# Fewer dummy matmuls, an earlier first weight magnitude, half of the first state sums moved behind two units, and eight matmuls split, in a scan that feeds a gated MLP

## The chip, the cores and the metric

The kernel runs on one core of a Trainium2 chip. The metric is the device time of one execution in microseconds (us); lower is better. The engines are PE (TensorE, with PEld for its weight loads), DVE (VectorE), ACT (ScalarE), POOL (GpSimd) and SP (SyncE, which here issues most of the DMAs).

## The reference

A scan over 768 tokens in chunks (4 batches, 8 heads, state 16, head width 32) gives an output that is laid out as 3072 rows of 256 values, and a gated MLP works on these rows. Cut to what matters:

```
log_a = log(clip(a, 1e-6, 1))                       # a: (4, 8, 768)
for each chunk of 32 tokens:
    cum = cumsum(log_a[chunk])
    L = exp(cum_i - cum_j) * (i >= j)
    M = (C @ B^T) * L
    y[chunk] = M @ x + (C @ state) * exp(cum)
    state = exp(sum(log_a)) * state + sum_j B_j x_j * exp(cum_end - cum_j)
x = y as (3072, 256)
out = (silu(x @ w_gate) * (x @ w_val)) @ w_out      # 256 -> 1536 -> 256
```

## The kernel before

**Tiling.** The tokens are taken in 6 blocks (`NB`) of 128 tokens, each of all four batches, so that a block has T = 512 columns. A block k goes through the scan first: the decays L (`scan_spread`, `scan_j`), the scores S (`scores`), the mix of the two (`mix`), the values, the carried states and the sums for new states on PE; the result is x of the block. Then it goes through 12 units f of the MLP. A unit computes gate and value (`gate_val`, m = 0 and 1, the tiles gv), silu on ACT, the product on DVE, and a high and a low half of that product (`hid_high`, `hid_low`) for the output sums (`project`, the tiles po).

**State sums.** The chunk of the scan is 64 tokens wide here, two pieces q of a block. Each piece has its own sum over B and x (`sums_of_pieces`, tile st for block 0). `apart` copies a piece's sum, by heads, from PSUM into the tile T, and `step` brings T of the second piece up to date with the first by the decays E. The values and carried matmuls of the first block stand in `values_first` and `carried_first`, and read T of the first piece alone; block 1 carries on from the second.

**Weights.** `w_gate` and `w_val` arrive as twelve pieces wg0 to wg11, one for each unit, `w_out` as wo0 to wo5. A piece of raw data (wg0r) is prepared in steps: its magnitude (ACT), range (POOL for the pieces in `FAR`, wg0 among them, else DVE), shift, sign and round (DVE), and a rest (ACT). The first nine units of block 0 (`WHOLE`) use the whole piece (wg0w) with the whole x (xf): two fp32 matmuls for each half unit m, which PE does as four passes. All others are three products of a high and a low half, six matmuls for each half unit (lines 652 to 654). Of the first piece, the gate half is rounded first, then the value half, in two operations each.

**Order.** A planner (`Plan`) takes all operations with an engine, a cost, a rank, needs and buffers, and puts them into an order by ranks, costs and due times (`due`). `plan.follow(...)` and the table `ORDER` fix chains of operations on an engine by hand. What comes out is one instruction stream for each engine, which that engine keeps to. All instructions are recorded by one helper, so every row says L191.

**Dummies.** `idle` issues matmuls whose result nobody reads: nine groups of four, 64 columns wide, at the start, and one 512 columns wide behind `e` (`IDLE`, lines 967 and 968). In the trace they write the tile rest.

**DMA.** SP loads B and C (bc), x and B by tokens (xb), the decays and the weight pieces wg. The clipped logarithms of all blocks are written to memory by ACT (clipped<-all), and L and E of the later blocks are loaded from there. POOL issues accumulating transfers, which make the low halves wg0l and so on, and xl of block 0.

Names of the tiles in rows: st, y and S are PSUM tiles of the scan; e is the spread decay that E is copied from.

Of the kernel before, what the change touches and what calls it, by code (L numbers as in the profile page):

```python
# [22 lines left out]
Q = 64  # L23
K = P // Q
T = BATCH * P
# [176 lines left out]
def scan_moe_kernel(ctx: ExitStack, tc, aj, an, bc, xb, wgv, wo, cst, own, first_e, out):  # L202
# [35 lines left out]
    def piece(q):  # L238
        return slice(Q * q, Q * q + Q)
# [180 lines left out]
    def sums_of_pieces(k, b):  # L420

        c = bl[k]
        if not b:
            tiles = c["tiles"][::2] if k else banks(k, "st", K)
            half = slice(BATCH * Q, None) if k else slice(0, BATCH * 2 * D)
            c["st"] = [t[:, half].rearrange("p (b c) -> p b c", c=2 * D) for t in tiles]
        for p in range(NP):
            for q in range(K - last(k, K - 1)):
                o = 2 * D * (p ^ b % 2)
                te.matmul(  # L430
                    c["st"][q][pair(p), b], c["Bj"][piece(q), b, pair(p)],
                    c["x"][piece(q), b, o : o + 2 * D], start=not k, stop=True, skip_group_check=k > 0,
                )

    def new_states(k):
        bl[k]["T"] = att.tile([P, K, BATCH, 2 * D], F32, tag="T", name=f"T{k}", bufs=2)
# [208 lines left out]
    def gate_val(k, f, m):  # L645
        t = hid.setdefault((k, f), {})["gv"[m]] = ps_mm.tile([P, T], F32, tag="mm", name=f"gv{k}_{f}_{m}")
        if not k and f < WHOLE:
            w = part[f]["w"].bitcast(F32).rearrange("p (a b c) -> p a b c", b=2, c=P)
            for kc in range(2):
                te.matmul(t, w[:, m, kc], whole[0][:, kc], start=not kc, stop=kc == 1)  # L650
            return
        runs = [(w, x, kc) for w, x in PASSES[not k] for kc in range(2)]
        for i, (w, x, kc) in enumerate(runs):
            te.matmul(t, w[f][:, m, kc], x[k][:, kc], start=i == 0, stop=i == 5)

    def silu(k, f):
        t = hid[k, f]
# [76 lines left out]
    def do(f, *a):  # L734
        return lambda *e: f(*a, *e)
# [78 lines left out]
    for k in range(NB):  # L814
# [44 lines left out]
        for bs in [(b,) for b in range(BATCH)] if not k else [range(BATCH)]:  # L859
            b, more = bs[-1], bs[0]  # L860
            n = len(bs)
            if not k:
                add("PE", 0.2, do(sums, 0, bs), -1.5, [("bt", 0), *([("st", 0, more - 1)] if more else [])], takes=[] if more else [("at", i) for i in st], uses=st, gives=("st", 0, b), kind="f")
            add("PE", 0.43 if n == 1 else 1.8, do(scores, k, bs), z + 3.5 if k else -1.9 + 0.1 * b, [("Cz", k)] + ([("S", k, more - 1)] if more else []), takes=[] if more else [("at" if k else "mm", i) for i in S], uses=[*S, CZ], gives=("S", k, b), kind="f", slack=SLACK)
        done = [("S", k, BATCH - 1)]
        add("-", 0.0, do(new_states, k), z + 2, behind("T"), takes=[("T", TT)], gives=("T", k))
        for q in range(len(st)):
            add([("Act", 0.65), ("DVE", 0.36)] if k else "Act", None if k else 0.65, do(apart, k, q) if k else do(apart, 0, q, "Act"), r + 2 if k and q else z + 4 + 0.5 * q, [("st", k, BATCH - 1), ("T", k)], uses=y if k else [st[q]], gives=("ap", k, q))
# [44 lines left out]
    for k in range(NB):  # L913
# [36 lines left out]
    plan.follow([  # L950
        *(("spread", b, 0) for b in range(BATCH)),
        *(("spread", b, 1) for b in range(BATCH)), *(("S", 0, b) for b in range(BATCH)),
        "e", *(("idle", 1, i) for i in range(len(IDLE[1]))), *(("st", 0, b) for b in range(BATCH)),
        ("vals", 0), ("y", 0, 0), ("vals", 1), ("y", 0, 1),
    ])
    plan.follow([("raw", i) for i in range(NW)])
    for steps in ORDER:
        plan.follow(steps)
    plan.follow([("clip", 0), ("clip", 1), "row"] + [("L", 0, b) if i else ("scan0", b) for b, i in halves] + [("bt", 0), ("M", 0, 0), ("M", 0, 1), ("ce", 0), ("M", 0, 2), ("M", 0, 3), ("shift", 0), ("sign", 0, "gate"), ("round", 0, "gate"), ("sign", 0), ("round", 0), ("step", 0, 1), ("range", 1)])
    plan.STAY = {"Act": 0.0, "PE": 0.3}  # L960
    plan.issue()

# [1 line left out]
CST = 2 + 2 * D  # L964
E_ROWS = slice(64, 64 + BATCH * H)
NA = NB * K * BATCH * H // P
IDLE = [-9.0] * 9, [-4.0]
IDLE_AFTER = [], ["e"]
FIRST_X = 0, 1, 2, 3, 4, 5
FETCH = dict(aj=10.0, an=35.0, bc=12.0, xb=31.0)  # L970
LATER = 3.0
WHOLE = 9
LAST = (5, 6, 9, 10, 11, 12)
MINUS = (3, 3, 4, 5, 5, 5, 10, 10, 10)
FEW = 8
# [2 lines left out]
SLOW = {2: 9.0}  # L978
ORDER = (
    ["few", ("raw", 2)],  # L980
    [("range", 2), "products", ("sign", 2)],
    [("mag", 6), "written e", ("rest", 7)],
    [("raw", 8), ("bc", 1), ("raw", 9), ("aj", 1), ("raw", 10), ("xb", 1), ("raw", 11), ("E", 1)],
    [("E", 0), ("mag", 0), ("ap", 0, 0), ("ap", 0, 1), ("rest", 0), *(("xf", i) for i in FIRST_X)],
    [("xf", 5), ("mag", 1), ("rest", 1), ("mag", 2), ("rest", 2), ("mag", 3)],
    [("round", 1), ("range", 2)],
    [("si", 0, 2), ("Cz", 1)],
# [64 lines left out]
```

## Time and profile before

| | us |
|---|---|
| median of 3 runs | 348.28 (347.66 to 348.31) |
| the profiled execution | 350.54 |
| its span, from the first instruction to the last | 348.5 |
| PE busy in the span | 341.0 |
| DVE busy | 224.4 |
| ACT busy | 124.8 |
| POOL busy | 45.1 |

The span is what the profiler's views count from; every time in a row is counted from its start. The profiled execution is one of its own and is not among the three timed runs. An engine that is busy for nearly the whole span sets the time in most places; the places where it is not busy are found in the timeline and in the chain of waits.

### The profile page before, as it was taken

The page shows a single profiled execution, that of the slowest core. Times are in us where ns is not written, and L with a number is a line of the kernel's source. Part 1 is how long each engine was busy: PE and PEld are TensorE (multiplying, and loading weights), DVE is VectorE, ACT ScalarE, POOL GpSimd, SP SyncE. Part 2 cuts the span into 40 slices and gives each one's busy share as a digit, 9 for nine tenths or more (in the row PEclk, how much of TensorE's full clock was granted, in tenths as well). Part 3 has the DMA queues.
Part 4 walks back from the last instruction along what each step waited for, and adds up shares of the span by engine and source line. Part 5 has one row for each costly group of instructions (what it writes and reads, how often), then busy time and mean ns, then how long its engine had stood idle before and what let it go on. Part 6 is the DMA issues. An engine that isn't in the chain of part 4 may idle for free.

```text
span 348.5 us, 7432 instructions
## 1 busy us (share of the span) xinstructions
PE 341.0 (98%) x3207; PEld 267.1 (77%) x3207; DVE 224.4 (64%) x398; ACT 124.8 (36%) x233; POOL 45.1 (13%) x36
## 2 busy tenths in 40 slices
PE   8979999999999999999999999999999999999996
PEld 7534448888878888888888888888888888888895
DVE  7869999969899882686472677445676430565320
ACT  4659958563355412222322222321212221222221
POOL 2366836410222000000000000000000000000000
PEclk9989999999999999999999999999999999999999
DMA  7799887992000951000471000391000000100001
GB/s 253 255 374 177 252 205 150 267 241 73 1 2 13 206 151 61 0 2 2 141 167 60 0 2 2 98 179 74 20 0 3 2 2 0 60 2 0 0 2 60
DMA packets 9983, 30.98 MB, mean 89 GB/s; under 512 B 1311, under 2 KB 2111, under 8 KB 9311
## 3 DMA queue, kind: packets, MB, share of 16 engines
q1 hardware_dynamic: 7192, 24.23, 24.8%
q0 software_dynamic: 1440, 2.88, 4.7%
q10 hardware_dynamic: 1319, 3.41, 3.3%
q8 instruction: 25, 0.41, 0.5%
q14 instruction: 7, 0.06, 0.1%
HBM read 24.28 MB, written 3.35 MB: 79 GB/s over the span
## 4 chain that ended last, share of the span: by engine, by line
PE 96%; DVE 2%; ACT 1%; DMA 1%; issue 0%; ACTq 0%; DVEq 0%
PE gv L191 59%; PE po L191 28%; PE y L191 4%; PE S L191 2%; PE a L191 1%; DVE wg1w L191 1%; DMA rows<-in_aj 1%; DVE wg0w L191 0%; PE e L191 0%; PE st L191 0%; DVE T L191 0%; DVE wg2w L191 0%; ACT T L191 0%; ACT xf L191 0%; ACT wg0r L191 0%
## 5 line engine op out<-in xcount | busy, mean ns | idle before, releaser
L191 DVE TENSOR_TENSOR sg<-gv,sg 128x512 f32<-128x512 f32 x72 | 49.5, 688 | 78.8 <-PE gv L191 75.7
L191 ACT ACTIVATE sg<-gv 128x512 f32<-128x512 f32 x72 | 42.8, 597 | 105.1 <-PE gv L191 105.1
L191 DVE TENSOR_TENSOR hh<-sg,hh 128x512 fp32r<-128x512 f32 x72 | 49.9, 695 | 13.2 <-ACT hh L191 11.7
L191 ACT CAST hh<-sg 128x512 fp32r<-128x512 f32 x31 | 19.3, 623 | 26.6 <-PE po L191 18.8
L191 DVE TENSOR_TENSOR_SCAN L<-L,dj 128x520 f32<-128x520 f32 x20 | 23.9, 1242 | 3.0 <-DMA L<-clipped 3.0
L191 ACT COPY ob<-po 128x512 f32<-128x512 f32 (+1 forms) x13 | 7.2, 555 | 48.6 <-PE po L191 48.1
L191 DVE CAST hh<-sg 128x512 fp32r<-128x512 f32 x41 | 17.3, 425 | 2.0 <-PE po L191 0.8
L191 PE MATMUL po<-hh,wo4h 128*128 128x512 f32 (+1 forms) x52 | 15.2, 376 | 0.0
L191 PE MATMUL po<-hh,wo2h 128*128 128x512 f32 (+1 forms) x52 | 15.2, 376 | 0.0
L191 PE MATMUL po<-hh,wo0h 128*128 128x512 f32 (+1 forms) x52 | 15.2, 375 | 0.0
L191 DVE TENSOR_TENSOR L<-S,L 128x512 f32<-128x512 f32 x24 | 15.0, 681 | 0.1
L191 PE MATMUL po<-hh,wo5h 128*128 128x512 f32 (+1 forms) x52 | 15.1, 373 | 0.0
L191 PE MATMUL po<-hh,wo1h 128*128 128x512 f32 (+1 forms) x52 | 15.0, 373 | 0.0
L191 PE MATMUL po<-hh,wo3h 128*128 128x512 f32 (+1 forms) x52 | 15.0, 373 | 0.0
L191 PEld LDWEIGHTS po<-hh,wo0h 128*128 128x128 f32 x52 | 9.5, 188 | 1.9 <-issue 0.2
L191 PEld LDWEIGHTS y<-L,xb 64*32 64x32 f32 x768 | 9.0, 109 | 2.6 <-issue 1.8
L191 PE MATMUL y<-L,xb 64*32 64x64 f32 x768 | 10.9, 231 | 0.0
L191 PEld LDWEIGHTS po<-hh,wo5h 128*128 128x128 f32 x52 | 9.5, 188 | 1.7
L191 PEld LDWEIGHTS po<-hh,wo1h 128*128 128x128 f32 x52 | 9.5, 188 | 1.7
L191 PEld LDWEIGHTS po<-hh,wo3h 128*128 128x128 f32 x52 | 9.5, 188 | 1.7
L191 PEld LDWEIGHTS po<-hh,wo4h 128*128 128x128 f32 x52 | 9.4, 188 | 1.8
L191 PEld LDWEIGHTS po<-hh,wo2h 128*128 128x128 f32 x52 | 9.4, 188 | 1.8
(302 smaller groups left out, 750.2 us busy)
## 6 DMA issues: line engine op xcount, KB each, us to landing
L<-clipped SPq DMA_DIRECT2D x10, 520.0 KB
xb<-in_xb SPq DMA_DIRECT2D x6, 768.0 KB, 10.5
bc<-in_bc SPq DMA_DIRECT2D x6, 512.0 KB, 3.3
out<-ob SPq DMA_DIRECT2D x11, 256.0 KB, 6.0
E<-clipped SPq DMA_DIRECT2D x5, 260.0 KB
wg0r<-in_wgv SPq DMA_DIRECT2D x1, 512.0 KB
wg1r<-in_wgv SPq DMA_DIRECT2D x1, 512.0 KB
wg2r<-in_wgv SPq DMA_DIRECT2D x1, 512.0 KB
```

What stands on the lines that cost most here:

```text
L191: ins = getattr(self.engine, name)(*a, **k)
```

## The change

Five things change. The nine groups of dummies at the start become four, 16 matmuls for 36. The state sums of block 0 are split by piece: `first_sums(0)` stays where both were, `first_sums(1)` has a PSUM bank of its own and needs the second half of unit 1, gv(0, 1, 1). The copy of the second piece into T (`apart`) and T's step follow later. ACT's list has the magnitude of wg0 ahead of E's copy. The third chain in `ORDER`, which places the list of products among DVE's steps, has other neighbours. In unit 6 of block 1 (`HALVED`), the middle four of six matmuls of each half unit are done in two halves of 256 columns: eight matmuls become sixteen.

```
-            tiles = c["tiles"][::2] if k else banks(k, "st", K)
-            half = slice(BATCH * Q, None) if k else slice(0, BATCH * 2 * D)
+            half = slice(BATCH * Q, None)
 ...
+    def first_sums(q):
+        t = banks(0, f"st{q}", 1)[0][:, : BATCH * 2 * D]
+        bl[0].setdefault("st", {})[q] = t.rearrange("p (b c) -> p b c", c=2 * D)
+        for b in range(BATCH):
+            for p in range(NP):
+                sum_of(0, b, q, p)
 ...
-            te.matmul(t, w[f][:, m, kc], x[k][:, kc], start=i == 0, stop=i == 5)
+            n = T // 2 if (k, f) == HALVED and 0 < i < 5 else T
+            for o in range(0, T, n):
+                te.matmul(t[:, o : o + n], w[f][:, m, kc], x[k][:, kc, o : o + n], start=i == 0, stop=i == 5)
 ...
+        for q in range(K if not k else 0):
+            add("PE", 0.45, do(first_sums, q), due(0, 1) if q else -1.5, [("bt", 0), *([("gv", 0, 1, 1)] if q else [])], takes=[("at", st[q])], uses=[st[q]], gives=("st", 0, q), kind="f")
 ...
-... r + 2 if k and q else z + 4 + 0.5 * q, [("st", k, BATCH - 1), ("T", k)], ...
+... r + 2 if k and q else due(0, 5) if q else z + 4, [("st", k, BATCH - 1 if k else q), ("T", k)], ...
 ...
-        "e", *(("idle", 1, i) for i in range(len(IDLE[1]))), *(("st", 0, b) for b in range(BATCH)),
+        "e", *(("idle", 1, i) for i in range(len(IDLE[1]))), ("st", 0, 0),
 ...
-    ... ("sign", 0), ("round", 0), ("step", 0, 1), ("range", 1)])
+    ... ("sign", 0), ("round", 0), ("range", 1)])
 ...
-IDLE = [-9.0] * 9, [-4.0]
+IDLE = [-9.0] * 4, [-4.0]
+HALVED = 1, 6
 ...
-    [("range", 2), "products", ("sign", 2)],
+    [("round", 3), "products", ("sign", 4)],
-    [("E", 0), ("mag", 0), ("ap", 0, 0), ("ap", 0, 1), ("rest", 0), *(("xf", i) for i in FIRST_X)],
+    [("mag", 0), ("E", 0), ("ap", 0, 0), ("rest", 0), *(("xf", i) for i in FIRST_X)],
```

On PE, the order around the first units, before (y is the scan's last work on block 0, and gv0_1_0 is the first half of unit 1 of block 0):

```order
L191 MATMUL y10_2_341<-bc0_98,T0_113 64x64 x2
L191 MATMUL gv0_0_0_397<-xf_142,wg0w_248 128x512 x2
L191 MATMUL gv0_0_1_414<-xf_142,wg0w_248 128x512 x2
L191 MATMUL gv0_1_0_426<-xf_142,wg1w_394 128x512 x2
L191 MATMUL gv0_1_1_438<-xf_142,wg1w_394 128x512 x2
L191 MATMUL gv0_2_0_456<-xf_142,wg2w_410 128x512 x2
L191 MATMUL gv0_2_1_472<-xf_142,wg2w_410 128x512 x2
```

And with the change (st10 is the sum of the second piece):

```order
L191 MATMUL y10_2_306<-bc0_98,T0_113 64x64 x2
L191 MATMUL gv0_0_0_357<-xf_140,wg0w_227 128x512 x2
L191 MATMUL gv0_0_1_372<-xf_140,wg0w_227 128x512 x2
L191 MATMUL gv0_1_0_384<-xf_140,wg1w_355 128x512 x2
L191 MATMUL gv0_1_1_395<-xf_140,wg1w_355 128x512 x2
L191 MATMUL st10_0_406<-xb0_100 32x64 x16
L191 MATMUL gv0_2_0_427<-xf_140,wg2w_367 128x512 x2
L191 MATMUL gv0_2_1_449<-xf_140,wg2w_367 128x512 x2
```

The 16 matmuls of the second piece's sums, which stood ahead of the values of block 0, now stand between units 1 and 2.

On DVE, the order behind the rounding of the first piece, before (ISA is the rounding, which the trace calls CUSTOM_DVE_ANT_0; T<-T,E is T's step, sg0_0 the product of unit 0):

```order
L191 ISA wg0w_248<-wg0r_138,wg0w_248 128x512
L191 SCALAR_TENSOR_TENSOR T0_113<-T0_113,E0_97 128x64 x4
L191 TENSOR_SCALAR wg1w_394<-wg1w_394 128x512 x2
L191 SCALAR_TENSOR_TENSOR wg1w_394<-wg1r_151,wg1w_394 128x512
L191 ISA wg1w_394<-wg1r_151,wg1w_394 128x1024
L191 TENSOR_SCALAR wg2w_410<-wg2w_410 128x512
L191 SCALAR_TENSOR_TENSOR all_102<-all_102,dn_82 128x195
L191 TENSOR_SCALAR wg2w_410<-wg2w_410 128x512
L191 TENSOR_TENSOR sg0_0_418<-gv0_0_1_414,sg0_0_418 128x512
```

And with the change, the same place up to the product of unit 1 (without the round of wg0, which is followed by the first of these rows):

```order
L191 TENSOR_SCALAR wg1w_355<-wg1w_355 128x512 x2
L191 SCALAR_TENSOR_TENSOR wg1w_355<-wg1r_143,wg1w_355 128x512
L191 ISA wg1w_355<-wg1r_143,wg1w_355 128x1024
L191 TENSOR_SCALAR wg2w_367<-wg2w_367 128x512 x2
L191 TENSOR_TENSOR sg0_0_375<-gv0_0_1_372,sg0_0_375 128x512
L191 SCALAR_TENSOR_TENSOR wg2w_367<-wg2r_167,wg2w_367 128x512
L191 ISA wg2w_367<-wg2r_167,wg2w_367 128x1024
L191 TENSOR_SCALAR wg3w_378<-wg3w_378 128x512
L191 SCALAR_TENSOR_TENSOR wg3w_378<-wg3r_172,wg3w_378 128x512
L191 ISA wg3w_378<-wg3r_172,wg3w_378 128x1024
L191 SCALAR_TENSOR_TENSOR all_102<-all_102,dn_82 128x195
L191 TENSOR_TENSOR sg0_1_398<-gv0_1_1_395,sg0_1_398 128x512
```

T's four steps are no longer between wg0 and wg1; they are the next row behind the last one here. The scan of all later blocks' logarithms (all<-all,dn) has moved from wg2 to behind wg3.

On POOL, the order of the ranges of wg8 to wg10 and of the accumulating DMAs, before:

```order
L191 TENSOR_SCALAR wg8w_490<-wg8w_490 128x512
L191 TENSOR_SCALAR wg9w_519<-wg9w_519 128x512
L191 DMA wg0l_511<-wg0w_248 128x512
L191 DMA wg1l_530<-wg1w_394 128x512
L191 TENSOR_SCALAR wg10w_555<-wg10w_555 128x512
L191 DMA wg2l_540<-wg2w_410 128x512
L191 DMA xl0_401<-xf_142 128x1024
```

And with the change:

```order
L191 TENSOR_SCALAR wg8w_461<-wg8w_461 128x512
L191 DMA wg0l_493<-wg0w_227 128x512
L191 DMA wg1l_499<-wg1w_355 128x512
L191 TENSOR_SCALAR wg9w_509<-wg9w_509 128x512
L191 DMA wg2l_522<-wg2w_367 128x512
L191 TENSOR_SCALAR wg10w_575<-wg10w_575 128x512
L191 DMA xl0_361<-xf_140 128x1024
```

Two DMAs have come ahead of the range of wg9, and one ahead of that of wg10. In block 1, one of the two copies of sums into T stands on DVE where it stood on ACT. SP's order of DMAs is the same.

## Rows read from the trace of the kernel before

**Rows 1.** The page: engines' busy us (share of the span) xinstructions; queues' packets, MB, share.
```profile
PE 341.0 (98%) x3207; PEld 267.1 (77%) x3207; DVE 224.4 (64%) x398; ACT 124.8 (36%) x233; POOL 45.1 (13%) x36
...
q8 instruction: 25, 0.41, 0.5%
```

**Rows 2.** The chain that ended last: start us, us, what.
```profile
2.83 0.42 DVE rows L191
...
18.40 0.69 DVE wg1w L191
19.10 0.76 DVE wg2w L191
19.97 20.74 PE gv L191 x44
...
225.81 16.32 PE po L191 x72
...
328.42 16.87 PE po L191 x108
```

**Rows 3.** Timeline of PE, 15.2 to 24: start, us, what [idle before <-releaser].
```profile
15.31 1.96 PE L191 MATMUL gv<-xf,wg0w 128*128 128x512 f32 x4 [0.38 <-ACT xf L191]
19.97 3.42 PE L191 MATMUL gv<-xf,wg0w 128*128 128x512 f32 x4 [2.71 <-DVE wg2w L191]
```

**Rows 4.** Timeline of DVE, 11 to 20.
```profile
13.70 0.43 DVE L191 TENSOR_SCALAR wg0w<-wg0w 128x512 int32<-128x512 int32 x1 [0.86 <-POOL wg0w L191]
...
15.88 0.86 DVE L191 SCALAR_TENSOR_TENSOR T<-T,E 128x64 f32<-128x64 f32 x4
```

**Rows 5.** Timeline of all engines and queues, 16 to 46.
```profile
16.68 0.19 PEld L191 LDWEIGHTS gv<-xf,wg0w 128*128 128x128 f32 x1 [0.24 <-issue]
...
25.31 0.35 ACTq L191 DMA_DIRECT2D clipped<-all  x1
...
37.55 1.02 POOL L191 DMA_DIRECT2D wg0l<-wg0w  x1
37.63 0.67 SPq L191 DMA_DIRECT2D E<-clipped  x1
```

**Rows 6.** Windows: busy us (xinstructions) by PE, PEld, DVE, ACT, POOL; clock; DMA; GB/s.
```profile
0.00:19.90 19.90, 15.69 (x347) 11.34 (x348) 16.22 (x36) 12.38 (x30) 6.38 (x12) 1.00 0.78 273
19.97:23.60 3.63, 3.63 (x5) 1.54 (x5) 0.77 (x3) 1.08 (x2) 3.63 (x3) 0.53 1.02 417
19.09:39.83 20.74, 19.86 (x43) 8.71 (x43) 16.89 (x30) 16.09 (x30) 15.78 (x9) 0.92 1.01 264
39.80:63.75 23.95, 23.95 (x382) 14.95 (x381) 23.88 (x43) 17.38 (x36) 13.91 (x11) 1.00 0.84 205
```

**Rows 7.** DMA view, 17.0 to 19.9: queue, packets, MB, share of 16 engines.
```profile
q8 instruction: 1, 0.02, 2.0%
```

**Rows 8.** DMA view, 19.9 to 37.9 (of its three queues, the first and the last).
```profile
q1 hardware_dynamic: 1065, 4.57, 99.8%
...
q14 instruction: 2, 0.02, 0.2%
```

**Rows 9.** Timelines of PE, at other places.
```profile
11.14 1.15 PE L191 MATMUL st<-xb 64*32 64x64 f32 x62
...
26.82 3.60 PE L191 MATMUL gv<-xf,wg2w 128*128 128x512 f32 x8
30.25 3.60 PE L191 MATMUL gv<-xf,wg3w 128*128 128x512 f32 x8
...
64.01 0.63 PE L191 MATMUL gv<-xh,wg0h 128*128 128x512 f32 x2
```

**Rows 10.** Timeline of ACT, 9 to 16.
```profile
10.99 0.69 ACT L191 ACTIVATE wg0w<-wg0r 128x512 f32<-128x512 f32 x1
12.62 0.88 ACT L191 ACTIVATE T<-st,cs 128x128 f32<-128x128 f32 x3
```

**Rows 11.** Timeline of DVE, 38 to 41: the first scans of block 1.
```profile
39.75 2.73 DVE L191 TENSOR_TENSOR_SCAN L<-L,dj 128x520 f32<-128x520 f32 x2
```

More of the change, by code (lines that the diff above doesn't have):

```diff
@@ L423, in sums_of_pieces, with sum_of @@
         if not b:
-            tiles = c["tiles"][::2] if k else banks(k, "st", K)
-            half = slice(BATCH * Q, None) if k else slice(0, BATCH * 2 * D)
-            c["st"] = [t[:, half].rearrange("p (b c) -> p b c", c=2 * D) for t in tiles]
+            half = slice(BATCH * Q, None)
+            c["st"] = [t[:, half].rearrange("p (b c) -> p b c", c=2 * D) for t in c["tiles"][::2]]
         for p in range(NP):
             for q in range(K - last(k, K - 1)):
[L429 to L433, printed above, removed]
+                sum_of(k, b, q, p)
+    def sum_of(k, b, q, p):
+        c = bl[k]
+        o = 2 * D * (p ^ b % 2)
+        te.matmul(
+            c["st"][q][pair(p), b], c["Bj"][piece(q), b, pair(p)],
+            c["x"][piece(q), b, o : o + 2 * D], start=not k, stop=True, skip_group_check=k > 0,
+        )
+    def first_sums(q):
[4 more added lines that the diff above has]
+                sum_of(0, b, q, p)
     def new_states(k):
@@ L861, in scan_moe_kernel @@
             n = len(bs)
-            if not k:
-                add("PE", 0.2, do(sums, 0, bs), -1.5, [("bt", 0), *([("st", 0, more - 1)] if more else [])], takes=[] if more else [("at", i) for i in st], uses=st, gives=("st", 0, b), kind="f")
             add("PE", 0.43 if n == 1 else 1.8, do(scores, k, bs), z + 3.5 if k else -1.9 + 0.1 * b, [("Cz", k)] + ([("S", k, more - 1)] if more else []), takes=[] if more else [("at" if k else "mm", i) for i in S], uses=[*S, CZ], gives=("S", k, b), kind="f", slack=SLACK)
@@ L866, in scan_moe_kernel @@
         add("-", 0.0, do(new_states, k), z + 2, behind("T"), takes=[("T", TT)], gives=("T", k))
+        for q in range(K if not k else 0):
+            add("PE", 0.45, do(first_sums, q), due(0, 1) if q else -1.5, [("bt", 0), *([("gv", 0, 1, 1)] if q else [])], takes=[("at", st[q])], uses=[st[q]], gives=("st", 0, q), kind="f")
         for q in range(len(st)):
-            add([("Act", 0.65), ("DVE", 0.36)] if k else "Act", None if k else 0.65, do(apart, k, q) if k else do(apart, 0, q, "Act"), r + 2 if k and q else z + 4 + 0.5 * q, [("st", k, BATCH - 1), ("T", k)], uses=y if k else [st[q]], gives=("ap", k, q))
+            add([("Act", 0.65), ("DVE", 0.36)] if k else "Act", None if k else 0.65, do(apart, k, q) if k else do(apart, 0, q, "Act"), r + 2 if k and q else due(0, 5) if q else z + 4, [("st", k, BATCH - 1 if k else q), ("T", k)], uses=y if k else [st[q]], gives=("ap", k, q))
         for p in range(NP):
@@ L958, in scan_moe_kernel @@
         plan.follow(steps)
-    plan.follow([("clip", 0), ("clip", 1), "row"] + [("L", 0, b) if i else ("scan0", b) for b, i in halves] + [("bt", 0), ("M", 0, 0), ("M", 0, 1), ("ce", 0), ("M", 0, 2), ("M", 0, 3), ("shift", 0), ("sign", 0, "gate"), ("round", 0, "gate"), ("sign", 0), ("round", 0), ("step", 0, 1), ("range", 1)])
+    plan.follow([("clip", 0), ("clip", 1), "row"] + [("L", 0, b) if i else ("scan0", b) for b, i in halves] + [("bt", 0), ("M", 0, 0), ("M", 0, 1), ("ce", 0), ("M", 0, 2), ("M", 0, 3), ("shift", 0), ("sign", 0, "gate"), ("round", 0, "gate"), ("sign", 0), ("round", 0), ("range", 1)])
     plan.STAY = {"Act": 0.0, "PE": 0.3}
```

## The prediction

> **What bounds the kernel now.** I read the page first: TensorE (PE) is busy 341.0 of 348.5 us, 98% [rows 1]. The chain of waits says where the other two per cent lie: from 19.97 us on it is PE work nearly to the end, and ahead of that it runs through the preparation of the first weight pieces on VectorE, wg1w, then wg2w [rows 2]. So whatever is won must be won before PE runs free, and kept until the next place where PE waits. The timeline of PE shows the one large hole: the first half of unit 0 (four passes) ends at 17.26, the next four start at 19.97, 2.71 us later [rows 3]. The view names wg2w's preparation as the releaser. But the matmul behind the hole reads xf and wg0w; it takes nothing from wg2. VectorE had rounded its weights before T's step, which stands behind that round, began at 15.88 [rows 4], and its weight load had already begun at 16.68 [rows 5]; the engine had its data and stood still. What was missing? The windows count 347 matmuls and 348 weight loads up to 19.90, so the one that stands still is about number 695 of PE's stream [rows 6]. The page has a queue that carries nothing but instructions: 25 packets, 0.41 MB; PE's 6414 instructions over 25 packets are 257 a packet [rows 1]. One such packet moved between 17.0 and 19.9, while the hole lasted [rows 7], and none at all between 19.9 and 37.9, when the data queue held the DMA engines for 99.8% of the time [rows 8]. I take the hole for PE waiting for its own instructions, which came late because the DMA engines were full. What follows it costs too: from 19.97 to 23.60 the granted clock is 0.53, near the lower of TensorE's two levels, after an idle stretch [rows 6]; the four passes took 3.42 us, where eight take 3.43 from one unit's start to the next later on (26.82 to 30.25) [rows 9], so 1.71 for four: 1.7 us more.
>
> [...]
>
> **The change, part by part.** *20 dummies fewer.* They stand ahead of `a`, and the chain comes to `a` through VectorE's work on its rows, to 3.25, and not through them [rows 2]: 0; with that cover gone, fewer dummies could only let it start earlier. What counts is that the stream gets 40 instructions shorter (a load and a matmul each).
>
> *Half of the first sums moved.* 64 passes took 1.15 us at 11.14 [rows 9]; 32 of them, with their 32 loads, go behind two units. ScalarE then has two copies of T instead of four ahead of its work on wg0 and xf: 0.88/3 = 0.3 each [rows 10], some 0.6 us on ScalarE, of which I let 0.4 count since it also waits for y. The hole's instruction, number 695, is now 40 + 64 = 104 further on. Counting eight instructions for each half unit, unit 0's second half, unit 1 and the 64 sums fill 88 of these, unit 2 the 16 left: it is now the first of unit 3.
>
> *Magnitude of wg0 first.* It ran at 10.99, behind E's copy [rows 10]. Its data can't be dated by a row; I take 0.9 us earlier, and from 0 to 1.3 as bounds. GpSimd's range of wg0 goes with it, and VectorE's shift waited 0.86 us for that range, from 12.84 to 13.70 [rows 4]; so 0.86 of the 0.9 count. Round 0 ends at 15.0 instead of 15.9. E's copy comes up to 0.3 later; its readers on VectorE have that slack.
>
> *T's step moved.* Its four pieces, 0.86 us on VectorE [rows 4], stood between round 0 and wg1's preparation. Now they stand behind product 1. Round 1 ended at 19.09 [rows 2]; 0.86 and half of the 0.86 above, less what ScalarE's magnitude of wg1 takes back, make 18.1. The copies' reader, the carried part of block 1, comes over 20 us later: 0 there.
>
> *So the start becomes:* unit 0 at 14.9 (15.31 less 0.4) to 18.3, at 3.43 us for a unit; unit 1 from 18.4 (round 1, 18.1, and a hop) to 21.8; the moved sums between 0 and 0.58, half of 1.15: I take 0.3; unit 2 at 22.1 where it was 26.82 [rows 9]. That is 4.7 us. The hole is gone if the packet lands before unit 3, 25.5. No row shows when it is asked for. If it is asked for one packet earlier in the stream, at number 439, that was within the sums, at about 11.4, before [rows 9], and it came by 19.9, 8.5 us; in the changed kernel that number comes at about 13, so it would land at 21.5, 4 us early. The other bound is in the rivals.
>
> *Two matmuls of four split in unit 6 of block 1.* Eight matmuls become sixteen halves. In the last sums, 36 whole and 72 half ones take 16.87 us, in the ones before 72 whole ones 16.32, 0.2267 each [rows 2]; so a half takes (16.87 - 36 x 0.2267)/72 = 0.121 and a pair 0.015 more than a whole: 8 x 0.015 = 0.12 us. [...]
>
> **What is late next.** The 4.7 us arrive at block 1's decays on VectorE, not at the end. From 19.09 to 39.83 VectorE is busy 16.89 of 20.74 us [rows 6]; from 18.1 on, with the step's 0.86, it could be through at 35.9 instead of 39.75, when the scans of L(1) begin [rows 11]. But L(1) must have landed. It has no landing row; the ends are 35.9 (already there) and 39.75 (it is what the scan waited for). The nearest row is ScalarE's write issued at 25.31, behind L's loads: its landing let SyncE issue E at 37.63 [rows 5]. I take 37.0: 2.75 earlier. From 39.80 to 63.75 VectorE is busy 23.88 of 23.95 us [rows 6], so its work there is the bound and PE's first pass on block 1 at 64.01 [rows 9] hangs on it, moving as it moves. One copy of T in block 1 now falls to VectorE, at most the 0.43 of a shift of 512 columns [rows 4]; I take 0.35: 64.01 - 2.75 + 0.35 = 61.6, a gain of 2.4, not 4.7: the rest goes into PE's wait for block 1. From there PE is the bound. Less 0.12 for the split: 2.3.
>
> **How it stands to the times.** The profiled run took 350.54 us, of it 348.5 in the span; the median of the timed runs is 348.28, 2.26 less. In the profiled run's own terms I forecast 348.2. Whether the timed runs have the low clock after the hole too, nothing shows; without it their scans would begin up to 1.6 us earlier and the gain be 2.3 - 1.6 = 0.7. I take a quarter of that off: 1.9, or **346.4 us**. With L landed early the scans start at 35.9, 3.85 earlier, and the gain is 3.85 - 0.35 - 0.12 = 3.4: 344.9.
>
> **Rivals.** *A: L(1) comes no earlier, or later.* On GpSimd the accumulating transfers of wg0l and wg1l, issued from 37.55 before [rows 5], now stand ahead of wg9's range instead of behind it, and so start earlier, in the stretch in which the DMA engines are full [rows 8]. For it: that share, 99.8%. Against: L's loads are queued well ahead of them, before the write of 25.31. If L lands at 39.75 as before, the gain is 0, and the copy and the split cost 0.35 + 0.12; less 0.1 to 0.2 where they are hidden: 348.6. It decides from a landing at 38.6 on, where under 0.7 is left.
>
> *B: the hole isn't instructions.* If the view is right and the matmul is let go by wg2's range, that ends 0.76 us behind round 1 [rows 2], at 18.9, and the second half starts at 19.0 instead of 19.97: 1.0 earlier, less 0.3 for the sums and 0.12: 347.7. For it: the releaser named, and the times fit (19.86 and 0.11). Against: that matmul reads nothing of wg2, and a hole that ends with an instruction packet needs no second reason. [...]
>
> *C, slower: the packet is late at its new place.* The rows show 18.0 us without a single packet, 19.9 to 37.9 [rows 8], under the same load that the changed kernel has when PE comes to unit 3. If the packet asked for at about 13 isn't through before this stretch, it comes when the data queue falls idle: PE stands from 25.5 to 37.9 and starts unit 3 at 38.0 at the earliest, where it was 30.25 [rows 9]: 7.8 us later, 356.0. It decides from a landing at 30.2 on; with 18 us of delay alone, 31, it would be about 1 us slower. Against: asked for no later than 1 us behind its time before, it should come nearly as then.
>
> [...]
>
> **How the numbers follow.** What this kernel's measurement can tell from no change is about 0.2%, 0.7 us (347.6 to 349.0). The forecast has a chance of 0.66 (faster 0.61, and 0.05 within 0.2%, where the timed runs have no low clock); A 0.12 (0.09 within, 0.03 slower, where the new transfers delay L past 39.75); B 0.10 (0.08 within, 0.02 faster); C 0.12, slower. Together: faster 0.63, same 0.22, slower 0.15. The range runs from 344.9 (L early) to 348.6 (A) and leaves out C and tails, some 0.2.
>
> **What would show it.** The profile after should have no hole in unit 0, a granted clock near 1 from 15 to 25, unit 2 at about 22, an instruction packet well before 25, the scans of L(1) at about 37 and PE on block 1's xh at 61.6. A hole ahead of unit 3 means C; one that has stayed in unit 0 and ends with wg2's range means B; scans that wait for L until 39 mean A. I'd be wrong altogether if PE reached block 1 two us early and lost them again further on, at weights of wg9 to wg11 or at xl, whose loads and accumulating transfers I have only bounded as unchanged.

## The result, and the profile after

The changed kernel takes 350.33 us in the median of 12 runs (348.98 to 351.02); the kernel before takes 348.29 beside it. The ratio is 1.0054, with an interval of 1.0039 to 1.0070: 2.0 us slower. The prediction was 346.4, in a range of 344.9 to 348.6, and faster. The time lies outside the range and on the other side.

The profiled execution after took 349.17 us, 1.4 less than the 350.54 of the profiled one before. Both numbers mislead, in opposite ways. The one after stands at the lower edge of its 12 runs. The one before stands 2.26 above the median of its own: it belongs to a few executions with a mean granted clock of 0.994 or 0.995, 6 of 35 of the kernel before and none of the 12 after. So both kernels were profiled once more. Four profiles, by the starts of PE's pieces, in us:

| | before, as shown | before again | after, as shown | after again |
|---|---|---|---|---|
| time of the execution | 350.54 | 348.33 | 349.17 | 350.39 |
| unit 0 | 15.31 | 15.75 | 15.39 | 15.52 |
| unit 1 | 23.19 | 21.15 | 19.13 | 21.05 |
| unit 2 | 26.82 | 24.58 | 23.31 | 25.16 |
| scores of block 1 | 40.64 | 38.41 | 37.24 | 39.09 |
| unit 10 | 56.63 | 54.40 | 54.44 | 55.71 |
| first pass of block 1's units | 64.01 | 61.79 | 62.45 | 63.71 |
| from there to the end of the span | 284.5 | 284.5 | 284.6 | 284.6 |

The last line tells that everything is decided in the first 64 us. The two columns that stand for the medians are "before again" and "after again". They differ by 1.92 us at the first pass of block 1, and by 0.1 behind it: together the 2.0 of the result.

The kernel before in its ordinary execution, PE's timeline (start, us, what). The hole of [rows 3] doesn't show; unit 0 takes 5.40 us up to unit 1 all the same, where unit 1 takes 3.43:

```profile
15.75 5.57 PE L191 MATMUL gv<-xf,wg0w 128*128 128x512 f32 x8
21.15 3.60 PE L191 MATMUL gv<-xf,wg1w 128*128 128x512 f32 x8
24.58 3.60 PE L191 MATMUL gv<-xf,wg2w 128*128 128x512 f32 x8
...
51.55 0.74 PE L191 MATMUL gv<-xh,wg9h 128*128 128x512 f32 x2
...
54.40 0.61 PE L191 MATMUL gv<-xh,wg10h 128*128 128x512 f32 x2
...
55.31 0.66 PE L191 MATMUL gv<-xh,wg10l 128*128 128x512 f32 x2
...
57.28 0.91 PE L191 MATMUL y<-bc,T 32*64 32x64 f32 x64
```

Its chain of waits from 14 to 64 us (start, us, what) is PE and nothing else, so from unit 0 on PE is the bound there:

```profile
15.82 22.66 PE gv L191 x48
38.48 1.14 PE S L191 x63
39.62 10.50 PE gv L191 x24
50.11 1.51 PE y L191 x97
```

But VectorE is close behind. It writes the low half of wg10 (wg10l) until 55.18, and PE takes it up at 55.31:

```profile
54.50 0.68 DVE L191 TENSOR_TENSOR wg10l<-wg10w,wg10h 128x512 fp32r<-128x512 f32 x1
```

The changed kernel near its median, PE's timeline:

```profile
15.52 5.70 PE L191 MATMUL gv<-xf,wg0w 128*128 128x512 f32 x8
21.05 3.60 PE L191 MATMUL gv<-xf,wg1w 128*128 128x512 f32 x8
24.58 0.65 PE L191 MATMUL st<-xb 64*32 64x64 f32 x32
25.16 3.70 PE L191 MATMUL gv<-xf,wg2w 128*128 128x512 f32 x8
...
52.23 0.72 PE L191 MATMUL gv<-xh,wg9h 128*128 128x512 f32 x2
...
55.71 0.73 PE L191 MATMUL gv<-xh,wg10h 128*128 128x512 f32 x2 [0.44 <-ACT wg10h L191]
...
57.19 0.74 PE L191 MATMUL gv<-xh,wg10l 128*128 128x512 f32 x2 [0.28 <-DVE wg10l L191]
...
59.23 0.91 PE L191 MATMUL y<-bc,T 32*64 32x64 f32 x64
```

Two things are to be seen. From unit 1 to unit 2 it is 4.11 us instead of 3.43: the moved sums lie on PE's unbroken run, 0.68. And PE now waits at unit 10, for the weights wg10 that VectorE rounds: 3.48 from unit 9 to unit 10 instead of 2.85, and 3.52 instead of 2.88 from there to the carried part, 1.27 together. With 0.23 won at unit 0's start and 0.2 lost on the way, that is the 1.92. The first profile of the changed kernel has the same waits, 3.82 and 3.52 us for these two stretches, though its unit 0 is quick. The chain of waits near the median leaves PE behind unit 0 and comes back from VectorE at wg10:

```profile
15.59 5.64 PE gv L191 x8
...
21.93 0.69 DVE wg2w L191
...
56.20 0.34 DVE T L191
56.53 0.61 DVE wg10l L191
57.19 2.11 PE gv L191 x8
```

Why VectorE is late is in its timeline. Before, ordinary execution:

```profile
13.85 0.43 DVE L191 TENSOR_SCALAR wg0w<-wg0w 128x512 int32<-128x512 int32 x1 [0.85 <-POOL wg0w L191]
...
16.02 0.87 DVE L191 SCALAR_TENSOR_TENSOR T<-T,E 128x64 f32<-128x64 f32 x4
...
19.58 0.56 DVE L191 TENSOR_TENSOR_SCAN all<-all,dn 128x195 f32<-128x195 f32 x1
20.06 0.40 DVE L191 TENSOR_SCALAR wg2w<-wg2w 128x512 int32<-128x512 int32 x1
21.42 0.69 DVE L191 TENSOR_TENSOR sg<-gv,sg 128x512 f32<-128x512 f32 x1 [0.96 <-PE gv L191]
```

And the changed kernel near its median:

```profile
14.58 0.42 DVE L191 CUSTOM_DVE_ANT_0 wg0w<-wg0r,wg0w 128x512 uint16<-128x512 uint16 x1
16.65 0.89 DVE L191 TENSOR_SCALAR wg1w<-wg1w 128x512 f32<-128x512 f32 x2 [1.65 <-ACT wg1w L191]
...
18.40 0.69 DVE L191 CUSTOM_DVE_ANT_0 wg1w<-wg1r,wg1w 128x1024 uint16<-128x1024 uint16 x1
19.01 0.88 DVE L191 TENSOR_SCALAR wg2w<-wg2w 128x512 f32<-128x512 f32 x2
21.32 0.69 DVE L191 TENSOR_TENSOR sg<-gv,sg 128x512 f32<-128x512 f32 x1 [1.43 <-PE gv L191]
```

Round 0 is over 1.1 us earlier, as forecast. But wg1 can't begin before ScalarE's magnitude of wg1, which stands behind the copies into xf, and so VectorE idles for 1.65 us where T's step had stood. Product 0 comes at 21.4 before and 21.3 now, since PE's unit 0 sets it. Ahead of it VectorE had done the step (0.86) and the scan of the later blocks (0.5) before; now it has done neither, and does both behind it. From there its run has no break of note (busy 34.77 of 35.20 us from 21.3 to 56.5): its waits from 12 us to the casts of xh are 3.1 us in all (1.65 and 1.43) where they were 1.8 (0.85 and 0.96). At the scans of block 1 it is 1.12 us later than before, and at wg10l 1.96. The rest is one longer instruction on wg10 (1.09 for 0.67), a few tenths more of that kind, and the copy of T that ScalarE had before:

```profile
56.12 0.41 DVE L191 TENSOR_TENSOR T<-y,cs 128x256 f32<-128x256 f32 x1
56.46 0.68 DVE L191 TENSOR_TENSOR wg10l<-wg10w,wg10h 128x512 fp32r<-128x512 f32 x1
```

### The profile page after: what moved, and what is told of

The parts are those of the page before. It is cut to its first block, busy times and chain, and to the rows that moved or that the text cites. A ratio compares the mean times of both kernels' runs of the same rounds, so it can differ in the third digit from the quotient of the medians.

```text
span 347.1 us, 7408 instructions
## 1 busy us (share of the span) xinstructions
PE 340.3 (98%) x3195; PEld 266.3 (77%) x3195; DVE 225.7 (65%) x399; ACT 124.3 (36%) x231; POOL 45.3 (13%) x36
## 3 DMA queue, kind: packets, MB, share of 16 engines
q0 software_dynamic: 1440, 2.88, 4.7%
## 4 chain that ended last, share of the span: by engine, by line
PE 97%; DVE 1%; DMA 1%; ACT 0%; issue 0%; ACTq 0%
PE gv L191 59%; PE po L191 29%; PE y L191 5%; PE S L191 2%; PE a L191 1%; DMA rows<-in_aj 1%; PE st L191 0%; PE e L191 0%; DVE sg L191 0%; DVE wg10l L191 0%; DVE wg11w L191 0%; PE rest L191 0%; DVE rows L191 0%; ACT ob L191 0%; DVE T L191 0%
## 5 line engine op out<-in xcount | busy, mean ns | idle before, releaser
L191 PE MATMUL po<-hh,wo4h 128*128 128x512 f32 (+1 forms) x52 | 15.2, 376 | 0.0
L191 PE MATMUL po<-hh,wo2h 128*128 128x512 f32 (+1 forms) x52 | 15.2, 375 | 0.0
L191 PE MATMUL po<-hh,wo0h 128*128 128x512 f32 (+1 forms) x52 | 15.2, 375 | 0.0
```

The lines of the kernel that those rows point to most:

```text
L191: ins = getattr(self.engine, name)(*a, **k)
```

## The experiments

Each variant was timed beside the kernel before; the ratio's interval stands behind each median. Medians of the kernel before were 348.01 to 348.29. A block of PE's instructions, in the expectations, is what one packet of the instruction queue is taken to bring: 257, the estimate that the prediction works out from [rows 1].

**The kernel before again.** 

> The kernel before, unchanged, run once more. Theory 1: the 2.71 us hole in unit 0 was an accident of the one profiled execution; most executions have none, so their spans are about 346.2 (the median 348.29 less the 2.04 us that lay outside the span) and a new profile shows unit 0 in one piece. Rival: the hole is in every execution and the timed runs differ by what lies outside the span: spans stay at 348.5 and the profile shows the hole again.

348.27 us in the median (0.9969 to 1.0019), span of the profiled execution 346.3. What stands in the hole's place is a slow unit 0. In the trace its passes start at 15.75, 16.76, 17.61, 18.47 and 19.44, and 0.43 apart from there on: 0.85 to 1.01 at first, half the pace. The trace's record of the granted clock begins at 19.27 only, with 1.00; the time ahead of it has no record, and the views count that as 1.00. In all 20 profiles the passes of unit 0 ahead of that first record start 0.85 us or more apart and those behind it 0.43 (the first of them 0.5), holes and the one pass in which it begins left out. In the first profile before, the record reads 0.50 from 20.16 to 23.57 and 1.00 on either side of that; in this stretch the passes start 0.85 apart too (20.63, 21.48, 22.33, 23.19), and 0.43 apart behind it (23.81, 24.24). So the slow ones ahead of the record have the pace that this trace shows at 0.50; the clock that they had is not on record. The record begins at 15.08 in the first profile of the changed kernel, which has no slow pass (0.43 apart from 15.93 on), and at 19.57 in the second.

So the hole wasn't gone, it was covered; theory 1 was wrong in that. The last paragraph on the experiments takes it up.

**The changed kernel again**, for a second profile. 

> The changed kernel once more, for a profile of an execution near its median (350.3) rather than near its lower edge (349.2, the profile so far). Theory 2 (a packet of PE's instructions for block 1 that is asked for at about 40 is served only when the DMA queues fall idle near 50, and in the longer executions later still): PE stands in the second half of the values of block 1 or in unit 9 or 10, and the first pass of block 1's units comes at about 63.7 instead of 62.45. Rival: VectorE's chain itself is over 1 us longer there, with xh at 62.7 instead of 61.4.

350.39: this is the column "after again". Theory 2 fell: PE's only waits from 15 to 64 us are the 0.44 and 0.28 for wg10. The rival held: xh came at 62.7 instead of 61.4. The two executions of the same program differ in unit 0 alone to begin with, 5.53 us, with slow passes until the clock's record begins at 19.57, against 3.74, with none and a record from 15.08 on; the wait for product 0 (1.43 against none) follows from it. The first profile of the changed kernel is of the lucky kind. Its 12 runs lie in two groups, five at 349.0 to 349.6 and seven at 350.3 to 351.0, which fits the two profiles; the timed runs have no record of unit 0.

**T's step alone**, in the kernel before:

```
-..., ("sign", 0), ("round", 0), ("step", 0, 1), ("range", 1)])
+..., ("sign", 0), ("round", 0), ("range", 1)])
 ORDER = (
+    [("pr", 0, 1), ("step", 0, 1)],
```

> The kernel before with one part of the change alone: T's step of block 0 behind product 1 instead of between round 0 and wg1. Theory 3 (VectorE is the bound up to block 1's first pass, and the step stood in a stretch in which VectorE waits anyway): VectorE waits 0.8 us for wg1's magnitude where the step stood and does the step later; xh and the time 0.8 later, 349.1. By the prediction's sum: the step's 0.86 us move out of the way of wg1, round 1 comes earlier, and the time falls or stays: 347.6 to 348.3.

348.99 (0.9994 to 1.0049) beside 348.22: 0.8 slower, the size that theory 3 gave, though the interval just reaches 1 and the profile, of a run at 348.58, has only 0.3 of it, at wg10l. VectorE's timeline shows the new wait where the step stood:

```profile
15.63 0.42 DVE L191 CUSTOM_DVE_ANT_0 wg0w<-wg0r,wg0w 128x512 uint16<-128x512 uint16 x1
16.82 0.89 DVE L191 TENSOR_SCALAR wg1w<-wg1w 128x512 f32<-128x512 f32 x2 [0.77 <-ACT wg1w L191]
...
21.38 0.69 DVE L191 TENSOR_TENSOR sg<-gv,sg 128x512 f32<-128x512 f32 x1 [0.98 <-PE gv L191]
```

**The sums and the step alone** (36 dummies, E's copy first, the scan's place and unit 6 as before). 

> The kernel before with the split and the gate of the first sums alone (the second half behind unit 1, its copy and T's step later); 36 dummies, E's copy first, the scan's place and unit 6 as before. Theory 4 (two things cost: the moved sums lie on PE's unbroken run from unit 0 on, 0.6 us, where they had lain in its waits before; and VectorE's step, 0.8, comes out of a wait into its unbroken run): 349.0 to 349.6. Rival (PE's stream alone, moved here by 64 instructions for 24 matmuls of units 0 and 1): a stretch of PE without instructions that the kernel before has not, and a time over 350.

349.09 (1.0012 to 1.0049) beside 348.01: 1.1 slower, inside theory 4's range. In its profile 4.11 us lie between units 1 and 2, and VectorE waits 0.70 for wg1's magnitude. This part by itself makes the kernel slower.

**The scan's place alone**, in the kernel before, and **put back**, in the changed one:

```
-    [("range", 2), "products", ("sign", 2)],
+    [("round", 3), "products", ("sign", 4)],
```

> The kernel before with the scan of the later blocks' logarithms (0.5 us of VectorE) behind wg3's round instead of within wg2's preparation, alone. Theory 3: it stood in VectorE's wait for product 0 and now stands behind it: 0.5 us slower, 348.8. Rival (only the step matters): 348.3.

> The changed kernel with that scan back within wg2's preparation, alone. Theory 3: 0.5 us off in the runs with slow passes in unit 0, less in the others: 349.8 to 350.0. Rival: 350.3.

Moved: 350.02 (1.0033 to 1.0088), 1.8 slower; the direction of theory 3, three times its size. The lowest runs are at 348.2 to 348.8, and four of 12 have the low mean clock of the first profile before (0.993 to 0.995). Why these came up more often isn't explained. Put back: 349.66 (1.0023 to 1.0060) against 350.33, 0.7 less, a little more than expected; the interval overlaps that of the changed kernel. In its profile the clock's record begins late, at 19.66, as in the changed kernel's second one, and PE's waits for wg10 are nearly gone: 3.05 us from unit 9 to unit 10 and 2.97 from there to the carried part. Block 1's first pass comes at 63.13 instead of 63.71, though unit 0 began 0.19 later.

**16 dummies alone**, in the kernel before. 

> The kernel before with 16 dummies alone. By the sum the dummies cost nothing: 348.3. If the places of instruction blocks decide: over 0.7 us either way, and a hole at another place of block 0, 40 instructions later in the stream than before (in unit 2 or 3 instead of unit 0).

349.57 (1.0004 to 1.0051), 1.3 slower. Not by a hole in block 0: the planner, which counts the dummies as work of PE, now puts product 0 ahead of wg2's shift and of the scan. VectorE's timeline:

```profile
19.12 0.42 DVE L191 TENSOR_SCALAR wg2w<-wg2w 128x512 f32<-128x512 f32 x1
21.38 0.69 DVE L191 TENSOR_TENSOR sg<-gv,sg 128x512 f32<-128x512 f32 x1 [1.84 <-PE gv L191]
21.99 0.42 DVE L191 TENSOR_SCALAR wg2w<-wg2w 128x512 int32<-128x512 int32 x1
22.32 0.56 DVE L191 TENSOR_TENSOR_SCAN all<-all,dn 128x195 f32<-128x195 f32 x1
```

The wait for product 0 is 1.84 instead of 0.96, and what had filled the difference comes behind it. PE then waits 0.25 us for wg2 and starts unit 10 at 55.51, 1.11 later than before; 0.34 of "issue" within block 1's scan work comes on top.

**The changed kernel with 36 dummies.** 

> The changed kernel with 36 dummies again, so PE's stream is 40 instructions longer ahead of everything and nothing else differs. Theory 1 (what slows the changed kernel is where PE's instruction blocks fall): the time moves by over 0.7 us, either way, and the spread of its runs (349.0 to 351.0) changes. Rival (it is the moved work, not the stream): the time stays at 350.3 with the same spread.

350.75 (1.0033 to 1.0082), 0.4 from 350.33 and with a similar spread (348.5 to 351.5): not the shift that its theory 1 asked for. One thing of it is in the profile: PE stands between two matmuls of one form, released by "issue",

```profile
52.18 0.32 PE L191 MATMUL y<-xb 64*32 64x64 f32 x9 [1.21 <-issue]
```

and by the DMA view an instruction packet moves between 49.9 and 51.0, ahead of its end. This one cost little: unit 9 starts later for it, and PE then has no wait for wg10 (2.87 us from unit 9 to unit 10).

**Without the split of unit 6.** 

> The changed kernel without the split of unit 6 of block 1: eight matmuls fewer, so 16 instructions fewer in the stream from there on. By the sum: 0.12 us faster, 350.2. If block boundaries behind unit 6 are what the split places: 0.5 us or more slower, with holes of PE behind block 1 that the changed kernel hasn't.

349.60 (1.0000 to 1.0050). The runs go from 348.1 to 350.8 and overlap the changed kernel's. From block 1's first pass to the end it is 284.53 against 284.64 us, so the split costs 0.11, as the sum had it; the other 0.6 of the medians is in what the executions made of the start.

**wg0's magnitude alone**, in the kernel before. 

> The kernel before with the magnitude of wg0 ahead of E's copy alone. Theory 3: VectorE's 0.85 us of waiting for GpSimd's range of wg0 goes, but it then waits for wg1's magnitude, which follows xf on ScalarE, by about as much, so round 1 and the time stay: 348.3 within 0.4. By the sum of the prediction: round 0 comes 0.86 earlier and the time falls by 0.4 to 0.8.

348.06 (0.9964 to 1.0010): no change, as theory 3 has it. This step of the change buys nothing by itself.

**Both magnitudes**, wg1's ahead of the last three copies into xf, in the changed kernel and in the kernel before:

```
-    ..., *(("xf", i) for i in FIRST_X)],
-    [("xf", 5), ("mag", 1), ("rest", 1), ...],
+    ..., *(("xf", i) for i in FIRST_X[:3]), ("mag", 1), *(("xf", i) for i in FIRST_X[3:])],
+    [("xf", 5), ("rest", 1), ...],
```

> The changed kernel with ScalarE's magnitude of wg1 ahead of the last three copies into xf, in a stretch where ScalarE waits anyway. Theory 3 (VectorE is the bound from 15 to 61 us, and the moved step left a hole of 1.46 us there, in which it waits for that magnitude): the hole is under 0.3, xh comes about 1.2 us earlier, and the time falls by 0.7 to 1.3 us, to 349.0 to 349.6. Rival (PE's instructions or a transfer set the end of block 0): the hole goes and the time stays at 350.3.

> The kernel before with both magnitudes moved, wg0's ahead of E's copy and wg1's ahead of the last three copies into xf; the sums, the step and the 36 dummies as before. Theory 3: both waits of VectorE go, 0.8 us of the time with them: 347.5. Rival (PE's slow passes in unit 0 set it): 348.3.

In the changed kernel 349.97 (1.0005 to 1.0051): three of 12 runs at 347.3 to 348.0, the others at 349.0 to 350.5. The hole of 1.46 us went, as expected, and 0.91 of it came back as a wait for product 0. That is less than theory 3 wanted for the median. The profile is of the lowest of the 12 runs, with a record of the clock from 14.85 on. Beside the first profile of the changed kernel, with its record from 15.08 on, it bears theory 3 out: PE's waits for wg10 are nearly gone (3.04 and 2.99 us), and block 1's first pass comes at 60.70 instead of 62.45. In the kernel before 349.51 (1.0008 to 1.0048), 1.2 slower where 0.8 faster was expected: both theories wrong. Its xh comes at 62.0, with 1.3 us of waits ahead of it on VectorE (0.43 and 0.89); the planner gave VectorE one of block 1's copies of T and a new order of products. I didn't take that apart.

**The sums put back** in the changed kernel (both halves ahead of the values, the step behind round 0), twice. 

> The changed kernel with both halves of the first sums ahead of the values again, both copies of T ahead of xf and T's step between round 0 and wg1; 16 dummies, wg0's magnitude ahead of E's copy, the scan's later place and the split stay. Theory 3: the step fills the wait again, 0.9 us off, and one copy of T is ScalarE's again, up to 0.35 more: 349.1 to 349.4. Rival (the sums' place itself, or PE's stream, is what costs): 350.3 or more.

> The changed kernel with the sums back, once more, for a profile near its median (352.25) rather than its lower edge (349.5). Theory 5 (a packet of PE's instructions lands late behind block 1's scan, where the profile so far stands 2.3 us between its carried part and unit 11): PE stands there for 4 us or more. Rival (VectorE is later still): no longer stretch there, xh at 63 instead of 60.5.

352.25 in the median of its ten runs; the interval (1.0054 to 1.0119) goes by the lower eight, with a median of 351.88. That is about 2.5 us more than was expected, and theory 5 fell too. In the execution at 352.06, with a record of the clock from 15.41 on, block 1's first pass comes at 61.58: 0.87 us ahead of the changed kernel's first profile, which is what theory 3 wanted, and better than in either profile of the kernel before. The loss is behind it. ScalarE waits 3.89 us for a piece of w_out, which stands ahead of a silu in its stream, and does the silu behind it, at 65.69:

```profile
65.13 0.65 ACT L191 ACTIVATE wo3r<-wo3r 128x512 int32<-128x512 uint32 x1 [3.89 <-DMA wo3r<-in_wo]
```

PE stands 1.85 us for that silu, and the granted clock is 0.57 in the 4 us afterwards (PE's timeline; then a window: us, busy us of PE, PEld, DVE, ACT, POOL, clock, DMA share, GB/s):

```profile
66.32 0.99 PE L191 MATMUL gv<-xh,wg1h 128*128 128x512 f32 x2 [1.85 <-ACT sg L191]
```

```profile
66.30:70.30 4.00, 3.98 (x10) 3.13 (x11) 4.00 (x7) 2.12 (x4) 2.08 (x1) 0.57 1.05 219
```

That is one execution, with a mean clock of 0.995. Four runs at 351.8 to 352.6 read 1.00, and what those lost isn't shown.

**All but sums, step and scan** (16 dummies, wg0's magnitude first, the split). 

> The kernel before with 16 dummies, wg0's magnitude first and the split of unit 6; sums, step and scan as before. The planner now puts product 0 ahead of wg2's shift and the scan, 0.9 us of VectorE, as it does with 16 dummies alone. Theory 4: those 0.9 us come out of the wait for product 0, 349.1 to 349.5. Rival (sums and step are the whole loss): 348.3.

351.01 (1.0044 to 1.0091), slower by 3.0 where theory 4 had 1.1 to 1.5. Unit 0 is quick in its profile (run at 350.40). PE waits 1.14 us for VectorE, twice 0.33 for L and 0.48 for wg10l, and stands as long again within block 1's carried part:

```profile
59.37 0.31 PE L191 MATMUL y<-L,xb 64*32 64x64 f32 x7 [1.15 <-issue]
```

An instruction packet moves between 57.0 and 58.2 and none between 52.5 and 57.0, when queues 0 and 10 hold the DMA engines (queue, packets, MB, share; 52.5 to 57.0):

```profile
q0 software_dynamic: 306, 0.54, 75.4%
q10 hardware_dynamic: 120, 0.48, 29.7%
```

In the changed kernel itself I saw no such hole.

**Unit 0 earlier**, in the kernel before: without the wide dummy behind e (`IDLE = [-9.0] * 9, []`), alone and with wg0's magnitude first.

> The kernel before with wg0's magnitude first and without the wide dummy of 0.6 us that stands between e and the first sums on PE. Theory 4 (from unit 0 on PE runs without a break to block 1, so what lets unit 0 begin earlier is won): unit 0 begins up to 0.5 earlier and the time is 347.6. Rival (unit 0's slow passes then last longer, or VectorE is the bound): 348.0 to 348.3.

> The kernel before without the wide dummy between e and the first sums, alone. Theory 4 (PE runs without a break from unit 0 to block 1, so an earlier unit 0 is won as it stands): unit 0 begins 0.2 to 0.5 earlier, VectorE's wait for GpSimd's range stays, 347.9. Rival (the range of wg0, which the gate half waits for, sets unit 0's start): 348.2.

> The kernel before with wg0's magnitude first and without the wide dummy, once more, for a narrower interval. Theory 4: 347.7, a ratio of 0.9985 to 0.9993. Rival (chance in the runs before): 348.2.

With both: 347.77 (0.9977 to 1.0002) and, again, 347.73 (0.9953 to 1.0003); with the dummy alone gone 348.10 (0.9968 to 1.0004). Unit 0 begins at 15.16 in the first of the three. All lie below the kernel before, by 0.1 to 0.5 us, and none of the intervals excludes 1: the best version of this study, and not shown to be faster.

**The hole of [rows 3] in the other traces.** Four variants that keep the start of the old stream have it too, in runs at ordinary times: the scan's place alone, wg0's magnitude alone, both magnitudes in the kernel before, and the wide dummy alone gone. PE's timeline in the first and the last of these:

```profile
15.28 1.95 PE L191 MATMUL gv<-xf,wg0w 128*128 128x512 f32 x4 [0.47 <-ACT xf L191]
19.02 1.88 PE L191 MATMUL gv<-xf,wg0w 128*128 128x512 f32 x4 [1.78 <-DVE wg1w L191]
```

```profile
15.42 2.38 PE L191 MATMUL gv<-xf,wg0w 128*128 128x512 f32 x5 [0.56 <-ACT xf L191]
19.02 1.45 PE L191 MATMUL gv<-xf,wg0w 128*128 128x512 f32 x3 [1.22 <-issue]
```

Without the wide dummy PE's stream is two instructions shorter, a load and a matmul, and the hole stands one pass later: at the same place of the stream. The releaser that the view names changes (wg2w, wg1w, "issue"). What doesn't change is the time since an instruction packet: by the trace's DMA records one ends at 18.62, 17.75, 17.95, 17.62 and 17.67 us in these five profiles, and the pass behind the hole starts 1.27 to 1.43 us later. The two late holes above end 1.35 and 1.42 us behind their packets. In the ordinary execution before, the packet ends at 18.05 and the fifth pass starts 1.39 later, at 19.44; at the slow pace it would have started at 19.32 anyway.

## Why the prediction was wrong, point by point

**What bounds the kernel.** This step failed first, in what the hole's removal is worth. The runs bear out the reading of the hole: in the five profiles with the old start it stands at one place of the stream and ends 1.27 to 1.43 us behind the end of an instruction packet, and the changed kernel has no such wait up to 66 us. When a packet is asked for, and why this one came so late, no trace shows: that full DMA engines held it up was my reading, and the 8.5 us from its request to its landing were an estimate on a supposition. But in the executions near the medians the clock's record begins at 19.27 and 19.57, PE's passes start 0.85 us or more apart until then and 0.43 behind it, and in the ordinary execution before the late packet holds PE up by 0.1 only. So the changed kernel starts unit 1 at 21.05 where it was 21.15. Where the record begins early and unit 0 has no slow pass, the change does win at unit 1: 19.13, against 20.31 to 21.10 in the four variants above. I costed the change on an execution that wasn't the ordinary one: in it the hole is followed by a stretch at a granted clock of 0.50, from 20.16 to 23.57. The sign was in the numbers, 350.54 against a median of 348.28; I named the 2.26 us and then gave the ordinary case a quarter of the weight. With its full weight my own sum said 0.7 us of gain, 347.6.

**wg1 earlier.** "0.86 and half of the 0.86 above, less what ScalarE's magnitude of wg1 takes back, make 18.1": the magnitude took back nearly all of it. Round 1 ended at 18.98 and 19.09, where it was 19.09 in [rows 2] and 19.33 in the ordinary execution. This term was mis-sized by 1.0 us. The step wasn't in wg1's way, it stood in a wait; moved, it left the wait behind and went into VectorE's unbroken run, 0.8 us by the medians with that edit alone, an interval that just reaches 1.

**The scan's place.** The prediction has no term for it, though the change names it: it was put at nothing without a reason. It moved 0.5 us of VectorE from ahead of product 0 into the run behind it, as the step's move did. Alone it made the kernel before 1.8 slower, more than that mechanism explains; put back in the changed kernel it took PE's waits for wg10 away but for 0.3.

**Where VectorE holds PE up.** The forecast had VectorE's run set block 1's first pass, through xh. In the executions near the medians PE comes to that pass from unit 11 without a wait. VectorE held it up earlier, at wg10: 1.27 us. That is the sign of being wrong that the prediction named, time lost again at weights of wg9 to wg11; the cause wasn't their loads or accumulating transfers but VectorE's own work, 1.96 us late there. The run from round 1 to the scans of L(1) was costed without any wait, 35.9 at the earliest; near the median the scans began at 38.90, after 1.43 us of waiting for product 0, which PE's unit 0 sets.

**The sums.** 0.3 was forecast, 0.58 to 0.68 was measured; and they had cost little where they stood, since unit 0's start moved by 0.23 only, for all that was taken out ahead of it.

**Unit 2 at 22.1.** It was 23.31 and, near the median, 25.16. Of 4.7 us forecast against [rows 9], 1.27 were left against the ordinary execution (24.58) where unit 0 had no slow pass, and nothing near the median.

**L(1).** It was no bound. SyncE issued E, which follows L's loads, at 34.44 in the ordinary execution before, long ahead of the scans at 37.78, and these follow VectorE's work without a gap. The forecast of 37.0 for the scans was near (37.73 and 38.90) for a wrong reason.

**Right in size.** The copy of T that came to VectorE (0.41, forecast 0.35), the split (0.11 for 0.12), and that what is won at the start would be cut down by VectorE ahead of block 1. The dummies were costed at nothing. Taken out alone they made the kernel before 1.3 slower, with another order on VectorE from the planner; how much of the 1.3 is that order isn't shown.

**The rivals.** None was it. A rests on a landing that never mattered, and its 348.6 is too low. B falls with the hole that moves along with the stream and ends at "issue". C didn't come: an instruction packet had ended at 18.36 in the changed kernel's first profile, and unit 3 began at 26.85 without a wait. The 18.0 us without a packet that C leans on don't say that one was waiting, since PE took only 43 matmuls and 43 loads from 19.09 to 39.83 [rows 6], a third of the 257 that I counted for a packet. The slower side needed a mechanism that I had in hand, VectorE's run of 23.88 in 23.95 us [rows 6], and used only for the gain.

**The sum as it turned out**, between the two executions near the medians: unit 0's start, -0.23; unit 0's length and later small delays, +0.2; the sums, +0.68; the waits for wg10, +1.27; the split, +0.1. That is 2.0. The parts taken one by one (1.1 for sums and step, 1.8 for the scan, 1.3 for the dummies) add up to more, and the change without sums, step and scan is 3.0 slower by itself: the planner gives each variant another order, and work that is moved competes for the same waits. So the sum stands on these two executions, one of each kernel, and the price of each part within the change isn't shown.

## What to carry to other kernels

Before costing anything on a profile, put the profiled execution's own time beside the median; where they differ by more than the gain in question, ask for another profile or give the ordinary case the weight. Work that stood in an engine's wait cost nothing there, and moving it "out of the way" put it into that engine's unbroken run (T's step alone: 0.8 us by the medians): for each step that is moved, look up what the engine would wait for in its old place and whether anything is left to fill it. Where a planner sets the order, an edit on one engine is also an edit of the others' order; take the other engine's rows from the order of both before costing it at nothing. And give every line of the change a term, even where it is nought.

## What the runs showed of the hardware

In all 20 profiles PE's passes in unit 0 start 0.85 us or more apart until the trace's record of the granted clock begins, with 1.00, and 0.43 apart behind that, holes and the stretch at 0.50 in the first profile before left out (20.16 to 23.57, 0.85 apart). The record begins at 13.33 and 19.27 us in the two profiles before, at 15.08 and 19.57 in the two after, and between 13.1 and 19.7 in all, in executions of nearly the same work; the views read 1.00 ahead of it. What sets the time at which the slow passes end wasn't found. In the changed kernel slow passes up to 19.57 come with a first pass of block 1 1.26 us later (63.71 against 62.45); in the kernel before it is about as late with slow passes as without (61.79, and 61.71 with wg0's magnitude first), since its hole stands where the slow passes would be.

Seven profiles have a hole of 1.15 to 2.71 us between two matmuls of one form, and in each it ends 1.27 to 1.43 us behind the end of an instruction packet; in the five that share the start of the stream it stands at the same place of it. I take these for PE waiting for its own instructions; no view names that. The releaser that the view names there was in some of them another engine's instruction, the work on wg2w or wg1w, which the pass doesn't read.
